# One burst instead of four for d^T g, and value products of two pairs of heads in one burst

## The chip, the cores and the metric

The kernel runs on one core of a Trainium2 chip. The metric is the device time of one execution in microseconds (us), from one launch that takes the inputs in HBM to the outputs in HBM. Everything is float32 at the interface.

## The reference

The inputs are q, k, v of 4 batches, 12 heads, 448 positions and 64 channels; three weights of a gated product (768 to 1536 and back), and a soft mixture of 8 experts with 4 slots each.

```python
scores = scale * np.matmul(q, k.transpose(0, 1, 3, 2)) - np.log(S)
attn = 1.0 / (1.0 + np.exp(-scores))
attn_out = np.matmul(attn, v)
x = attn_out.transpose(0, 2, 1, 3).reshape(B * S, H * D)
x = ((x @ w_a) * (x @ w_b)) @ w_out
logits = x @ phi
d = softmax(logits over tokens); slot_input = d.T @ x
slot_out[e] = np.maximum(slot_input[e] @ w1[e], 0.0) @ w2[e]   # 8 experts, 4 slots each
c = softmax(logits over slots)
return c @ slot_out
```

## The kernel before

The product with w_out is never formed for the tokens. With g = (x w_a) * (x w_b), the logits are g times wphi, where wphi = w_out phi is made once, and the slots' inputs are (d^T g) w_out. So for each batch the kernel needs the attention, the two products that give g (1536 rows in 12 blocks of 128, transposed: features on partitions, 448 tokens along), the logits, the softmax numerators d, and d^T g, which is added into an accumulator `acc` of 32 slots by 1536 features.

**Attention.** The generator `att` walks over 24 pairs of heads (g = 0 to 23; 6 pairs are a batch). For a pair, `emit_TK` and `emit_TQ` transpose k and q on TensorE (L144) and split each into a rounded part and a rest (h and l). `emit_S` computes the scores of a chunk of 112 keys for both heads with three products of the parts (L176), into two PSUM tiles of the tag `sc`, which has 4 buffers, and ScalarE turns each into a tile `a` with the sigmoid (L179). `emit_PV` multiplies the values of both heads with the eight tiles `a` of the pair (L189): plain float32 products of 64 columns each, the two heads beside each other in the array, into one `sc` tile. `emit_x` evacuates that tile as `xh` (ScalarE, L200) and `xl` (VectorE, L201).

**The two products.** The generator `ab` goes through 12 blocks of features of a batch. For each of w_a and w_b it runs three sets of 6 matmuls of 128 x 128 by 448 columns (L480; xh times wh, xl times wh, xh times wl) in the fp32r type, and yields after every 3 of them. There are two PSUM tiles of the tag `ab`. ScalarE copies the first product out (L489), VectorE multiplies the second with it (L492). The halves wh and wl of the weights are made ahead by VectorE (L407) and GpSimd (L408) from an f32 copy that the sync engine's queue loads (L399).

**What fills in between.** The instruction order on each engine is the order in which the code emits. While `ab` runs for batch b, `att_to` advances `att` for batch b+2 by units of cost: each `yield` of `att` says what the emitted piece counts (a transpose 430, two chunks of scores 1600, the value products 3200), and pieces are emitted while the sum lies below the share of `ab` that is done. After each set of 6 matmuls `fill_step` takes one step of the list `fill`: `group` (logits of four blocks, L443, and the transposes of g to token-major tiles `gk`, L457) and `LG` (the softmax over tokens: `logits`, L514; `tokens`, L548; then `dg`, L557). `dg` computes d^T g of the batch: for each of 4 chunks of 112 tokens, four float32 matmuls with 32 columns side by side, first over two thirds of the features (256 columns along), then over the last third (128 along). It yields after every second chunk, so a batch's d^T g stands in four pieces with a set of `ab` between them. `last_LG` does the last batch, where nothing is left to put between.

**After the products.** When `ab` of the last batch is done, the memory of its weights and inputs is opened to the loads of w_out and of the expert weights (`pump`, L688), and the expert stages run (L764 to L840).

Of the kernel before, what the change touches and what calls it, by code (L numbers as in the profile page):

```python
# [9 lines left out]
F32 = mybir.dt.float32  # L10
# [8 lines left out]
B, H, S, D = 4, 12, 448, 64  # L19
DM, FF, NS, NE, F = 768, 1536, 32, 8, 1024  # L20
C = 4
T = S // C
# [3 lines left out]
NP = H // 2  # L26
# [7 lines left out]
def body(ctx, tc, q, k, v, w_a, w_b, w_out, phi, w1, w2, out):  # L34
    nc = tc.nc
    pe, act, dve, pool, sp = nc.tensor, nc.scalar, nc.vector, nc.gpsimd, nc.sync

    const = ctx.enter_context(tc.tile_pool(name="const", bufs=1, side="left"))
    stat = ctx.enter_context(tc.tile_pool(name="stat", bufs=2, side="left"))
    ps_ctx, ab_ctx, x0_ctx, cv_ctx, at_ctx = (ctx.enter_context(ExitStack()) for _ in range(5))  # L40
    lgp = ctx.enter_context(tc.tile_pool(name="lgp", bufs=1, side="left"))
    gkp = ctx.enter_context(tc.tile_pool(name="gkp", bufs=1, side="left"))
    abp = ab_ctx.enter_context(tc.tile_pool(name="abp", bufs=1, side="left"))
# [1 line left out]
    x0p = x0_ctx.enter_context(tc.tile_pool(name="x0p", bufs=1, side="left"))  # L45
    cvp = cv_ctx.enter_context(tc.tile_pool(name="cvp", bufs=1, side="left"))
    atp = at_ctx.enter_context(tc.tile_pool(name="atp", bufs=1, side="right"))
    drp = ctx.enter_context(tc.tile_pool(name="drp", bufs=1, space=bass.MemoryType.DRAM))
    psp = ps_ctx.enter_context(tc.tile_pool(name="psp", bufs=1, space=PSUM))

# [2 lines left out]
    def ps_tile(tag, shape, bufs):  # L53
        return psp.tile(shape, F32, tag=tag, name=tag, bufs=bufs)
# [93 lines left out]
    def emit_TK(g):  # L148
        if g >= B * NP:
            return  # L150
        tk = transposed(g, "k", ms())
        if g == 0:
            tq = transposed(g, "q", ms())
        split_heads(g, "k", tk, dve.tensor_copy)
        if g == 0:
            split_heads(g, "q", tq, act.copy)

    def emit_TQ(g):
        if g >= B * NP:
            return  # L160
        split_heads(g, "q", transposed(g, "q", ms()),
                    dve.tensor_copy)
# [3 lines left out]
    def emit_S(g, chunks):  # L166

        (kh, kl), (qh, ql) = stk[g]["k"], stk[g]["q"]
        for c in chunks:
            ab = g < NP and c % 2  # L170
            sc = [ps_tile("ab" if ab else "sc", [T, S], 2 if ab else 4) for _ in range(2)]
            cs = slice(c * T, (c + 1) * T)
            for i, (kx, qx) in enumerate(((kh, qh), (kl, qh), (kh, ql))):
                for h in range(2):
                    r = slice(64 * h, 64 * h + 64)
                    pe.matmul(sc[h], kx[r, cs], qx[r], start=(i == 0), stop=(i == 2))  # L176
            for h in range(2):
                a = atp.tile([T, S], F32, tag="a", name="a", bufs=11)
                act.activation(a, sc[h], AF.Sigmoid, bias=nlog[:T], scale=1.0 / math.sqrt(D))  # L179
                a_t[g, h, c] = a  # L180

# [2 lines left out]
    def emit_PV(g, cs):  # L184
        if cs[0] == 0:
            pv_t[g] = ps_tile("sc", [128, S], 4)
        for c in cs:
            for h in range(2):
                pe.matmul(pv_t[g][64 * h:64 * h + 64], qkv_t["v", g][:, h, c, :], a_t.pop((g, h, c)),  # L189
                          start=(c == 0), stop=(c == C - 1))  # L190
# [3 lines left out]
    def emit_x(g):  # L194
        pv = pv_t.pop(g)
        qkv_t.pop(("v", g))
        b, kk = divmod(g, NP)
        xh = (x0p, x1p)[b % 2].tile([128, S], F32R, tag=f"xh{kk}", name=f"xh{kk}")
        xl = (x0p, x1p)[b % 2].tile([128, S], F32R, tag=f"xl{kk}", name=f"xl{kk}")
        act.activation(xh, pv, AF.Copy)  # L200
        dve.tensor_tensor(xl, pv, xh.bitcast(F32), op=ALU.subtract)  # L201
        xt[g] = (xh, xl)
        load_qkv(g + 3, "v")

    def att():

        emit_TK(0)
        yield 860
        for g in range(B * NP + 1):
            more = g < B * NP  # L210
            first = ((0, 1) if g == 0 else (0,) if g < NP else ()) if more else ()
            if g:
                emit_TK(g + 1)
                yield 430
            for c in first:
                emit_S(g, (c,))
                yield 800
            if g:
                emit_PV(g - 1, (0, 1, 2, 3))
                emit_x(g - 1)  # L220
                yield 3200
            elif more:
                emit_TK(g + 1)
                yield 430
            if more and g >= NP:
                emit_S(g, (0, 1))
                yield 1600
                emit_TQ(g + 1)
                yield 430
                emit_S(g, (2, 3))  # L230
                yield 1600
            elif more:
                emit_TQ(g + 1)
                yield 430
                for c in range(len(first), C):
                    emit_S(g, (c,))
                    yield 800
# [313 lines left out]
    def dg(b, dtok, gp, groups):  # L551

        gk = gtok[b, 2][:, None] if groups == (2,) else gk_01[:T].rearrange("p g (c n) -> p g c n", c=C)
        o = gp.rearrange("p (g n) -> p g n", g=3)[:, groups[0]:groups[-1] + 1]
        for c in range(C):
            for j in range(4):
                pe.matmul(o[32 * j:32 * j + 32], dtok[:, c], gk[:, :, c, j * 128:(j + 1) * 128],  # L557
                          start=(c == 0), stop=(c == C - 1))
            if c % 2:
                yield  # L560

    def LG(b):
        t = run["lsd2"] if b == B - 2 else ls_d
        run["lsd"] = t[:, :S], t[:, S:2 * S]
        dtok = t[:T, 2 * S:2 * S + C * NS].rearrange("p (c s) -> p c s", c=C)
        yield
        yield from logits(b)
        yield
        ltok = stat.tile([T, C, NS], F32, tag="ltok", name="ltok", bufs=1)
        tokens(run["lsd"][0], ltok)  # L570
        sp.dma_start(out=clog32[:, :, b], in_=ltok)
        yield
        tokens(run["lsd"][1], dtok)
        yield
        gp = ms((128, FF // 4))
        for groups in ((0, 1), (2,)):
            yield from dg(b, dtok, gp, groups)
        if b:
            dve.scalar_tensor_tensor(acc, acc, run["al"], gp, op0=ALU.mult, op1=ALU.add)
        else:  # L580
            dve.tensor_copy(acc, gp)
        yield
        if b == B - 2:
            run.pop("lsd2")
            open_slots(e1, [1])
            open_slots(gkp, [0])

    def last_LG():

        run["ms"], run["lsd"] = 0, (lps, gT_all[3])  # L590
        lg, gr = logits(B - 1), group(B - 1, 2, (act.copy, dve.tensor_copy, act.copy, act.copy))
        next(gr)
        next(lg)
        next(lg)
        next(gr)
        next(lg)
        next(gr)
        dtok = stat.tile([T, C, NS], F32, tag="ltok", name="dtok", bufs=1)
        tokens(run["lsd"][1], dtok)
        for _ in gr:  # L600
            pass
        next(lg, None)
        gp = ms((128, FF // 4))
        for groups in ((0, 1), (2,)):
            for _ in dg(B - 1, dtok, gp, groups):
                pass
        dve.scalar_tensor_tensor(acc, acc, run["al"], gp, op0=ALU.mult, op1=ALU.add)
        gt = ms((128, FF // 4))
        for gi in range(3):
            cs = slice(gi * 128, (gi + 1) * 128)  # L610
            pe.transpose(gt[:, cs], acc[:, cs], ident)
        act.copy(GT, gt)
        dve.tensor_scalar(rs, run["s"], 1e-9, None, op0=ALU.add)
        dve.reciprocal(out=rs, in_=rs)
# [99 lines left out]
    for b in range(B):  # L714
        if b == 1:
            cv_ctx.close()
        if b == B - 1:
            at_ctx.close()
            x0_ctx.close()
            e1 = ctx.enter_context(tc.tile_pool(name="e1", bufs=1, side="right"))  # L720
            run["banks"] = 1
            open_slots(e1, range(2, NE1))
            run["lsd2"] = e1.tile([128, 2048], F32, tag="e11", name="lsd2")
            run["wr"] = e1.tile([128, 2048], F32, tag="e10", name="wr")
            load_w(LAST + 2)
            load_w(LAST + 3)
        base = att_state[0]
        goal = NP * PAIR
        for i, frac in enumerate(ab(b)):
            if b < B - 1:  # L730
                att_to(base + goal * min(1.0, frac * 1.02))
            elif i % 6 == 3:
                pump()
        if b < B - 1:
            att_pairs((b + 2) * NP)
        for kk in range(NP):
            xt.pop(b * NP + kk)
        if b < B - 1:
            fill.append(LG(b))
# [39 lines left out]
    for n in range(0, len(order1), 4):  # L779
        _, g, x, _ = order1[n]  # L780
# [22 lines left out]
    for n in range(0, len(order2), 4):  # L803
        _, g, x, _ = order2[n]
# [62 lines left out]
```

## Time and profile before

| | |
|---|---|
| time, median of 3 runs (lowest to highest) | 742.64 us (740.13 to 744.14) |
| time of the profiled execution | 740.87 us |
| its span, first to last instruction | 738.8 us |
| TensorE matmul busy | 691.9 us, 94% |
| VectorE, ScalarE, GpSimd busy | 314.5, 271.4, 246.3 us |
| mean granted TensorE clock | 0.98 of full speed |

The profiled execution's own time is 2.07 us longer than its span. Times of instructions overlap on TensorE: the matmuls are pipelined, so what a stretch of matmuls costs is read from its start to the start of what follows, and not from its duration.

### The profile page before, as it was taken

To read this page: it belongs to the slowest core of one execution; us is meant where nothing else is said; L and a number is where in the kernel's file an instruction comes from. 1 tells how busy PE (TensorE), PEld (TensorE's weight loads), DVE (VectorE), ACT (ScalarE), POOL (GpSimd) and SP (SyncE) were. 2 spreads that over 40 slices of the span, in tenths; PEclk is the share of its full clock that TensorE was granted. 3 is DMA by queue.
4 is the path that set the end of the run, shared out by engine and by line. 5 is a ranking of instruction groups with operands and counts; after the bars stand their busy time and mean duration, and the time that the engine had idled before them with its cause. 6 is when DMAs were issued, how large, how long until landed. Compare 5 with 4: busy or idle time off the path is not lost.

```text
span 738.8 us, 10842 instructions
## 1 busy us (share of the span) xinstructions
PE 691.9 (94%) x4231; PEld 486.8 (66%) x4231; DVE 314.5 (43%) x452; ACT 271.4 (37%) x469; POOL 246.3 (33%) x151
## 2 busy tenths in 40 slices
PE   6999998999999999999999999999999998996682
PEld 4446767777777777777767777877888896441121
DVE  3457998899853233333333343331322232210013
ACT  4778778779643423232234222321201102110012
POOL 0006766666662322332322212322334442000000
PEclk9999999999999999999999999999999999999896
DMA  8857999899961332233323322210879927999958
GB/s 215 185 159 212 308 293 279 276 287 280 300 203 45 112 113 80 69 111 112 107 69 88 110 68 86 73 58 1 306 256 330 376 88 288 388 415 416 416 197 294
DMA packets 102930, 148.99 MB, mean 202 GB/s; under 512 B 51168, under 2 KB 76512, under 8 KB 99808
## 3 DMA queue, kind: packets, MB, share of 16 engines
q1 hardware_dynamic: 102880, 148.31, 61.3%
q8 instruction: 33, 0.54, 0.3%
q14 instruction: 17, 0.14, 0.1%
HBM read 128.46 MB, written 19.83 MB: 201 GB/s over the span
## 4 chain that ended last, share of the span: by engine, by line
PE 76%; DMA 11%; DVE 6%; ACT 4%; issue 1%; POOL 0%; SPq 0%; DVEq 0%; ACTq 0%; POOLq 0%
PE ab L480 44%; PE sc L189 9%; DMA e<-in_moe_w 7%; PE sc L176 7%; PE sc L784 3%; PE ms L144 3%; PE ms L457 2%; DVE gk L305 2%; ACT a L179 2%; PE ms L443 1%; PE ms L557 1%; DMA kn<-in_k 1%; PE ab L176 1%; DVE gk L304 1%; DMA wr_cv<-in_moe_w_a 1%
## 5 line engine op out<-in xcount | busy, mean ns | idle before, releaser
L408 POOL TENSOR_TENSOR wl<-wr_all,wh 128x768 fp32r<-128x768 f32 x50 | 92.2, 1845 | 209.1 <-DVE wh L407 159.3
L480 PE MATMUL ab<-xh,wl 128*128 128x448 f32 x576 | 144.9, 379 | 0.0
L480 PE MATMUL ab<-xh,wh 128*128 128x448 f32 x576 | 141.4, 376 | 1.4 <-ACT wh L407 1.4
L480 PE MATMUL ab<-xl,wh 128*128 128x448 f32 x576 | 135.9, 370 | 0.0
L480 PEld LDWEIGHTS ab<-xh,wh 128*128 128x128 f32 x576 | 103.4, 188 | 25.8 <-issue 15.8
L480 PEld LDWEIGHTS ab<-xh,wl 128*128 128x128 f32 x576 | 102.7, 188 | 22.4 <-issue 12.8
L179 ACT ACTIVATE a<-sc,nlog 112x448 f32<-112x448 f32 x168 | 93.7, 640 | 64.9 <-PE sc L176 64.7
L480 PEld LDWEIGHTS ab<-xl,wh 128*128 128x128 f32 x576 | 106.1, 188 | 13.5 <-issue 5.2
L310 POOL TENSOR_TENSOR w<-gk,cy 128x768 int32<-128x768 int32 x36 | 66.2, 1839 | 101.3 <-DVE gk L305 76.9
L492 DVE TENSOR_TENSOR misc<-misc,ab 128x448 f32<-128x448 f32 x48 | 29.6, 616 | 119.6 <-PE ab L480 119.6
L189 PE MATMUL sc<-a,vn 112*64 112x448 f32 x384 | 78.7, 553 | 0.0
L489 ACT COPY misc<-ab 128x448 f32<-128x448 f32 x48 | 25.9, 539 | 133.9 <-PE ab L480 133.9
L408 POOL TENSOR_TENSOR wl<-wr,wh 128x768 fp32r<-128x768 f32 x22 | 40.5, 1839 | 54.6 <-DVE wh L407 45.7
L407 DVE CAST wh<-wr_all 128x768 fp32r<-128x768 f32 x50 | 40.9, 820 | 28.9 <-issue 16.7
L189 PEld LDWEIGHTS sc<-a,vn 112*64 112x64 f32 x384 | 25.8, 139 | 41.4 <-issue 38.6
L808 PE MATMUL sc<-e,gk 128*32 128x384 f32 x240 | 37.1, 589 | 14.2 <-DMA e<-in_moe_w 13.9
L200 ACT ACTIVATE xh<-sc 128x448 fp32r<-128x448 f32 x24 | 13.1, 545 | 89.9 <-PE sc L189 89.9
L408 POOL TENSOR_TENSOR wl<-w,wh 128x768 fp32r<-128x768 f32 x24 | 44.9, 1870 | 3.1 <-ACT wh L407 3.1
L201 DVE TENSOR_TENSOR xl<-sc,xh 128x448 fp32r<-128x448 f32 x24 | 14.9, 622 | 58.9 <-ACT xh L200 58.9
L303 DVE TENSOR_SCALAR mf<-gk 128x768 f32<-128x768 f32 x36 | 34.1, 946 | 9.3 <-ACT gk L292 9.0
L808 PEld LDWEIGHTS sc<-e,gk 128*32 128x32 f32 x240 | 10.5, 125 | 39.9 <-DMA e<-in_moe_w 27.8
L176 PE MATMUL sc<-qh,kh 64*112 64x448 f32 x168 | 35.3, 415 | 0.6 <-ACT qh L137 0.6
(166 smaller groups left out, 764.7 us busy)
## 6 DMA issues: line engine op xcount, KB each, us to landing
e<-in_moe_w SPq DMA_DIRECT2D x23, 1024.0 KB, 7.3
e<-in_moe_w SPq DMA_DIRECT2D x27, 768.0 KB, 15.1
wr_all<-ab SPq DMA_DIRECT2D x50, 384.0 KB, 3.5
wr_cv<-in_moe_w_a SPq DMA_DIRECT2D x12, 768.0 KB, 6.9
wr_all<-in_moe_w_b SPq DMA_DIRECT2D x12, 768.0 KB, 7.0
wr_all<-in_moe_w_out SPq DMA_DIRECT2D x12, 768.0 KB, 7.2
ab<-w SPq DMA_DIRECT2D x24, 384.0 KB, 7.4
wr<-ab SPq DMA_DIRECT2D x22, 384.0 KB, 4.2
```

Of the source, the lines that this page charges most:

```text
L144: pe.transpose(t[:, c * T:(c + 1) * T], a[:, c].rearrange("p h d -> p (h d)"), ident[:T, :T])
L176: pe.matmul(sc[h], kx[r, cs], qx[r], start=(i == 0), stop=(i == 2))
L179: act.activation(a, sc[h], AF.Sigmoid, bias=nlog[:T], scale=1.0 / math.sqrt(D))
L189: pe.matmul(pv_t[g][64 * h:64 * h + 64], qkv_t["v", g][:, h, c, :], a_t.pop((g, h, c)), start=(c == 0), stop=(c == C - 1))
L303: dve.tensor_scalar(mf, m, LOW, HIGH, op0=ALU.max, op1=ALU.min)
L310: pool.tensor_tensor(thirds(w), m.bitcast(I32), thirds(cy_t.pop(x)), op=ALU.add)
L407: rnd(wh, t)
L408: pool.tensor_tensor(wl, t, wh.bitcast(F32), op=ALU.subtract)
L480: pe.matmul(t, w[:, kk * 128:(kk + 1) * 128], xt[b * NP + kk][xi], start=(s == 0 and kk == 0), stop=(s == 2 and kk == KD - 1))
L489: act.copy(gT_all[n % 5], t)
L492: dve.tensor_tensor(g, g, t, op=ALU.mult)
L808: pe.matmul(sps[h][32 * j:32 * j + 32], hT[:, 2 * x + i, 2 * j + g], ring[order2[n + j]][0][:, i, c0:c0 + w], start=(g == 0 and x == 0 and ...
```

## The change

Two things are changed. `dg` loses its yields: the 32 matmuls of a batch's d^T g are issued in a row. And from the pair g = 13 on, `att` emits no value products at odd g; at even g it emits those of g-2 and g-1 in a row, then both evacuations, and counts 6400. So that the eight tiles `a` of a pair can live until then, the odd pairs from 13 on take theirs from a new pool of 8 buffers (`a2`), opened when the first phase's pool `cvp` is closed.

```diff
+    more_a = {}
...
-                a = atp.tile([T, S], F32, tag="a", name="a", bufs=11)
+                a = (more_a["pool"].tile([T, S], F32, tag="a2", name="a2", bufs=8) if g >= 2 * NP and g % 2 else
+                     atp.tile([T, S], F32, tag="a", name="a", bufs=11))
...
-            if g:
+            if g > 2 * NP:
+
+                if g % 2 == 0:
+                    emit_PV(g - 2, (0, 1, 2, 3))
+                    emit_PV(g - 1, (0, 1, 2, 3))
+                    emit_x(g - 2)
+                    emit_x(g - 1)
+                    yield 6400
+            elif g:
                 emit_PV(g - 1, (0, 1, 2, 3))
                 emit_x(g - 1)
                 yield 3200
...
-            if c % 2:
-                yield
...
         for groups in ((0, 1), (2,)):
-            yield from dg(b, dtok, gp, groups)
+            dg(b, dtok, gp, groups)
...
         if b == 1:
             cv_ctx.close()
+            more_a["pool"] = ma_ctx.enter_context(tc.tile_pool(name="map", bufs=1, side="left"))
         if b == B - 1:
+            ma_ctx.close()
             at_ctx.close()
```

On TensorE the programs are the same up to the place where the value products of pair 12 stood, at the start of batch 1's `ab`. This is the order there before; numbered names are tiles, and xh, xl, wh, wl are the parts of inputs and weights.

```order
L480 MATMUL ab<-xh_2118,wh_2500 128x448
L480 MATMUL ab<-xh_2381,wh_2500 128x448
L189 MATMUL sc<-a,vn 64x448 x8
L480 MATMUL ab<-xl_942,wh_2500 128x448
L480 MATMUL ab<-xl_1214,wh_2500 128x448
L480 MATMUL ab<-xl_1527,wh_2500 128x448
```

This is TensorE's order at the first double burst now, 39 matmuls of `ab` later (L490 is the line of the products, L191 that of the value products, L567 that of d^T g).

```order
L490 MATMUL ab<-xl_1527,wh_2631 128x448
L191 MATMUL sc<-a,vn 64x448 x8
L191 MATMUL sc<-a_2643,vn 64x448
L191 MATMUL sc<-a_2645,vn 64x448
L191 MATMUL sc<-a_2655,vn 64x448
L191 MATMUL sc<-a_2657,vn 64x448
L191 MATMUL sc<-a_2712,vn 64x448
L191 MATMUL sc<-a_2714,vn 64x448
L191 MATMUL sc<-a_2724,vn 64x448
L191 MATMUL sc<-a_2726,vn 64x448
L490 MATMUL ab<-xl_1806,wh_2631 128x448
```

The eight matmuls of one pair have become sixteen in a row; the second eight read the tiles of the new pool. On TensorE, the last two pieces of d^T g of batch 0 stood like this before:

```order
L480 MATMUL ab<-xh_1805,wh_2653 128x448
L480 MATMUL ab<-xh_2118,wh_2653 128x448
L480 MATMUL ab<-xh_2381,wh_2653 128x448
L557 MATMUL ms<-gk_96,ls_d 32x128 x8
L480 MATMUL ab<-xl_942,wh_2653 128x448
L480 MATMUL ab<-xl_1214,wh_2653 128x448
L480 MATMUL ab<-xl_1527,wh_2653 128x448
L480 MATMUL ab<-xl_1806,wh_2653 128x448
L480 MATMUL ab<-xl_2119,wh_2653 128x448
L480 MATMUL ab<-xl_2382,wh_2653 128x448
L557 MATMUL ms<-gk_96,ls_d 32x128 x8
```

And all of d^T g of batch 0 stands like this now, again on TensorE:

```order
L490 MATMUL ab<-xl_1806,wh_2631 128x448
L490 MATMUL ab<-xl_2119,wh_2631 128x448
L490 MATMUL ab<-xl_2382,wh_2631 128x448
L567 MATMUL ms<-gk_95,ls_d 32x256 x16
L567 MATMUL ms<-gk_96,ls_d 32x128 x16
L490 MATMUL ab<-xh_941,wl_2632 128x448
L490 MATMUL ab<-xh_1213,wl_2632 128x448
```

The four pieces are one. On ScalarE, the evacuation of a pair stood before (here pair 13, with its last sigmoids ahead and the copy of an `ab` tile behind):

```order
L179 ACTIVATE a<-sc,nlog 112x448 x4
L489 COPY misc<-ab 128x448
L179 ACTIVATE a<-sc,nlog 112x448 x4
L200 ACTIVATE xh_2878<-sc 128x448
L489 COPY misc<-ab 128x448
```

ScalarE's order at the first double burst now:

```order
L181 ACTIVATE a_2712<-sc,nlog 112x448
L181 ACTIVATE a_2714<-sc,nlog 112x448
L181 ACTIVATE a_2724<-sc,nlog 112x448
L181 ACTIVATE a_2726<-sc,nlog 112x448
L202 ACTIVATE xh_2801<-sc 128x448
L202 ACTIVATE xh_2807<-sc 128x448
L499 COPY misc<-ab 128x448 x2
```

The two evacuations now follow each other, and the copies of `ab` tiles stand behind both.

## Rows read from the trace of the kernel before

**Rows 1.** The page's head, its second part and its chain by engine and line:
```profile
span 738.8 us, 10842 instructions
PE 691.9 (94%) x4231; PEld 486.8 (66%) x4231; DVE 314.5 (43%) x452; ACT 271.4 (37%) x469; POOL 246.3 (33%) x151
...
PE 76%; DMA 11%; DVE 6%; ACT 4%; issue 1%; POOL 0%; SPq 0%; DVEq 0%; ACTq 0%; POOLq 0%
```

**Rows 2.** Busy us by stretch: PE, PEld, DVE, ACT, POOL, clock, DMA share, GB/s:
```profile
200.00:340.00 140.00, 139.43 (x844) 102.90 (x843) 53.81 (x82) 47.12 (x84) 47.90 (x26) 1.00 0.35 104
340.00:480.00 140.00, 140.00 (x833) 105.66 (x832) 49.10 (x78) 42.52 (x78) 44.20 (x24) 1.00 0.31 92
480.00:616.00 136.00, 136.00 (x756) 113.79 (x754) 36.58 (x62) 20.30 (x38) 51.52 (x28) 1.00 0.56 199
623.00:626.00 3.00, 2.82 (x65) 1.85 (x64) 0.11 (x1) 0.76 (x2) 2.06 (x13) 1.00 1.02 429
640.00:650.00 10.00, 10.00 (x99) 3.04 (x92) 0.00 (x0) 0.53 (x1) 0.00 (x0) 1.00 1.01 417
```

**Rows 3.** All waits of PE between 200 and 618 us: line, waited for, us, times, longest:
```profile
PE ms L335 <- ACT wT L336: 0.6, 1, 0.6
```

**Rows 4.** Timeline of PE around one pair's value products: start, us, engine, line, operation:
```profile
357.00 0.85 PE L480 MATMUL ab<-xh,wl 128*128 128x448 f32 x3
357.78 3.23 PE L189 MATMUL sc<-a,vn 112*64 112x448 f32 x16
360.94 0.87 PE L480 MATMUL ab<-xh,wl 128*128 128x448 f32 x3
361.65 1.38 PE L480 MATMUL ab<-xh,wh 128*128 128x448 f32 x6
362.87 1.38 PE L480 MATMUL ab<-xl,wh 128*128 128x448 f32 x6
```

**Rows 5.** The same burst cut off at 358.5 and at 359.2 us:
```profile
357.78 0.97 PE L189 MATMUL sc<-a,vn 112*64 112x448 f32 x4
357.78 1.72 PE L189 MATMUL sc<-a,vn 112*64 112x448 f32 x8
```

**Rows 6.** Timeline of PE, d^T g of batch 0 in its four pieces:
```profile
253.36 1.07 PE L557 MATMUL ms<-gk,ls_d 112*32 112x256 f32 x16
254.37 0.88 PE L480 MATMUL ab<-xh,wl 128*128 128x448 f32 x3
...
256.20 1.07 PE L557 MATMUL ms<-gk,ls_d 112*32 112x256 f32 x16
257.20 0.86 PE L480 MATMUL ab<-xh,wh 128*128 128x448 f32 x3
...
260.20 0.64 PE L557 MATMUL ms<-gk,ls_d 112*32 112x128 f32 x16
260.77 1.48 PE L480 MATMUL ab<-xl,wh 128*128 128x448 f32 x6
262.18 0.64 PE L557 MATMUL ms<-gk,ls_d 112*32 112x128 f32 x16
262.75 1.49 PE L480 MATMUL ab<-xh,wl 128*128 128x448 f32 x6
```

**Rows 7.** Timeline of PE, d^T g of the last batch, already in one piece:
```profile
623.02 2.81 PE L557 MATMUL ab<-gk,dtok 112*32 112x256 f32 x64
```

**Rows 8.** Timeline of ACT around the value products of Rows 4; brackets give idle time before:
```profile
353.02 2.21 ACT L179 ACTIVATE a<-sc,nlog 112x448 f32<-112x448 f32 x4 [4.04 <-PE sc L176]
...
361.08 0.55 ACT L200 ACTIVATE xh<-sc 128x448 fp32r<-128x448 f32 x1 [5.43 <-PE sc L189]
```

**Rows 9.** The queue's waits (SP) from 500 us to the end:
```profile
SPq L399 <- PE ab L480: 22.2, 1, 22.2
```

**Rows 10.** The chain that ended last, in order of time, its late part:
```profile
594.47 21.89 PE ab L480 x108
...
660.02 15.04 DMA e<-in_moe_w
```

More of the change, by code (lines that the diff above doesn't have):

```diff
@@ L39, in body @@
     stat = ctx.enter_context(tc.tile_pool(name="stat", bufs=2, side="left"))
-    ps_ctx, ab_ctx, x0_ctx, cv_ctx, at_ctx = (ctx.enter_context(ExitStack()) for _ in range(5))
+    ps_ctx, ab_ctx, x0_ctx, cv_ctx, ma_ctx, at_ctx = (ctx.enter_context(ExitStack()) for _ in range(6))
     lgp = ctx.enter_context(tc.tile_pool(name="lgp", bufs=1, side="left"))
@@ L604, in last_LG @@
         for groups in ((0, 1), (2,)):
-            for _ in dg(B - 1, dtok, gp, groups):
-                pass
+            dg(B - 1, dtok, gp, groups)
         dve.scalar_tensor_tensor(acc, acc, run["al"], gp, op0=ALU.mult, op1=ALU.add)
```

## The prediction

> **What bounds the kernel now.** I read the page's head and its chain first. TensorE is busy for 691.9 us of a span of 738.8 us, and 76% of the chain that ended last is its matmuls [rows 1]. Everything that the change touches lies between the start of batch 1's products (pair 12's value products) and the first blocks of the last batch (d^T g of batch 2). So I took the table of busy time by stretch next: from 200 to 616 us TensorE is busy for 139.4 of 140, 140 of 140 and 136 of 136 us, at a granted clock of 1.00, while VectorE, ScalarE and GpSimd are each busy for at most 54 us of any of these stretches [rows 2]. The list of its waits from 200 to 618 us has a single entry, 0.6 us [rows 3]. So in this stretch nothing is waited for: whatever TensorE is spared there, the end comes earlier by, as long as no new wait arises. And whatever is to be spared must lie inside "busy" time, since there is no idle time.
>
> That it does is seen in the timeline, read from start to start. Six matmuls of the products that stand inside a long run take 1.22 us (361.65 to 362.87), 0.203 us each [rows 4]. Three of them that stand between a transpose and a burst of value products take 0.78 us (357.00 to 357.78) where 0.61 would do, and the first three behind that burst take 0.71 us (360.94 to 361.65) [rows 4]. Six that stand between two pieces of d^T g take 1.41 us (260.77 to 262.18) where 1.22 would do [rows 6]. So a stretch of the products that is cut out by other work costs 0.17 to 0.19 us more than its matmuls: about 0.10 us on entering it, the rest on leaving it. The bursts have a fixed part too, below.
>
> What follows the products is tied to them. The queue that loads the last expert weights waits for a matmul of the products, once for 22.2 us [rows 9], and the chain goes from the products (594.47 us) to the transfers of the expert weights, whose first link in it begins at 660.02 us [rows 10]. Those transfers are the bound at the end, but they are let go by TensorE, so they start earlier by what it is spared; I count no loss there.
>
> **The change, part by part.** *d^T g in one burst, three times* (batches 0 to 2; the last batch had no work between its pieces before). The four pieces of batch 0 take 1.01, 1.00, 0.57 and 0.57 us from start to start, 3.15 us [rows 6]. What one burst takes is in the trace, because the last batch does the same 64 records in one: 2.81 us of duration [rows 7], at a clock of 1.00 [rows 2]. A piece's duration is some 0.06 us more than its start-to-start time (1.07 against 1.01, [rows 6]), so I take 2.75 us: 0.40 us less per batch, 1.2 us for three. This term has no lower bound of its own, since the operation was seen.
>
> *Value products of two pairs in one burst, six times* (pairs 12 to 23, twelve bursts become six). Cut off at two points, the burst shows 4 records after 0.97 us, 8 after 1.72 and 16 after 3.23 us [rows 4, 5]; from 8 to 16 records that is 0.378 us per two (one of each head), so eight of those are 3.02 us. The burst takes 3.16 us from start to start (357.78 to 360.94) [rows 4], hence a fixed part of 0.14 us, and a double burst should take about 6.18 us instead of 6.32. Six times 0.14 is 0.84 us. The trace has no two pairs behind each other: if the second pair pays its own beginning, this is nothing; at the rate of the first eight records (1.72 less 0.97 us for four, 3.00 us in all [rows 5]) the fixed part is 0.16 us, 0.96 us for six. I take 0.84, since within a burst the rate does not change when a new chunk starts.
>
> *The stretches between.* Taking out six bursts and nine pieces would join fifteen pairs of stretches. But the rest of the attention now falls at other places between the sets. So I counted in the two orders: 166 stretches of the products between other work before, 153 now, 13 fewer with the same number of matmuls. At 0.18 us each, the middle of what the rows show, that is 2.34 us. If only the entering cost goes (0.10 us), it is 1.3 us; with all fifteen at 0.19 us it is 2.85 us.
>
> *What the delay costs elsewhere.* Delaying an even pair's value products by one pair keeps eight more `a` tiles alive, for which there is the new pool. In the order, from the last scores of a pair to the burst that needs them lie 21 matmuls of the products at every double burst; before there were 18 or 21. Moreover the burst begins with the older pair, so the younger pair's sigmoids have some 3 us more. Before, the last four sigmoids ended at 355.23 us (353.02 and 2.21) and the burst began at 357.78 [rows 4, 8]: 2.5 us to spare, over 5 now. Between scores and scores there are 18 or 21 matmuls, as before, so the four `sc` buffers are turned over no faster; a double burst takes two of them and, by its 6400 units, leaves as much of the products behind it as two single ones. The loads of v come in twos behind the burst and have a pair's time before they are wanted. The sync engine's queue puts nothing of its own ahead of them that TensorE waits for. I cost all this at nothing. If that cover were gone, a late tile of sigmoids would cost up to one sigmoid pass of four, 2.2 us [rows 8], at each burst.
>
> The sum: 1.2 + 0.84 + 2.34 = 4.4 us. Its bounds are 1.2 + 0 + 1.3 = 2.5 us and 1.2 + 0.96 + 2.85 = 5.0 us. The profiled execution took 740.87 us (span 738.8 and 2.07 around it), so an execution like it would take 736.5. The median of the three runs, 742.64, lies 1.8 us above that execution; the forecast for a median is 742.64 - 4.4 = **738.2 us**, with 737.6 to 740.1 from the bounds.
>
> **The rivals.** *Half of it.* The second pair of a burst pays its own beginning and a seam costs only its entry: 2.5 us, 740.1 us, within what can be told from no change (about 0.5%, 3.7 us). For it speaks that 13 seams at 0.18 are an average of differing neighbours, and that the double burst is not in the trace. Against it speaks that leaving the products towards a burst was measured apart from entering (0.78 for three matmuls in front of the burst, 0.71 behind it [rows 4]).
>
> *Nothing.* A seam might cost nothing in truth, the extra time being one of how the records' starts are put down, so that it reappears elsewhere; then only order changes, and the time stays at about 742.6 us. Against it: the extra tenths add up in a span that has no idle time, and the one-piece d^T g is shorter than the four by 0.40 us in the same trace [rows 6, 7]. The Trainium skill, "TensorE: Matmul & The Clock Gate", section "Step-by-step: what each phase is for", says that the drain of one matmul overlaps the fill of the next, so that matmuls in a stream follow each other at the pace of their columns; taken for any two matmuls, that makes every seam free and this rival true, with a sum of 0 where the rows give 4.4. This trace disagrees where the shape or type changes: 1.41 us in place of 1.22 [rows 6]. The same skill's "TensorEngine Tiling (Array Packing)", section "Key Properties", says that a change of tiling mode drains the engine, which is nearer to what these rows show.
>
> *Slower.* ScalarE takes its instructions in order. The evacuations of both pairs now stand one behind the other, and copies of `ab` tiles stand behind them; during a double burst ScalarE is held for some 6 us. If the copy of a tile is among what is held, TensorE finds no free `ab` tile after the burst and waits until the second evacuation (0.55 us) and the copy (0.55 us) are done [rows 8], some 1.2 us with the signals; at six bursts that is 7.2 us, less the 4.4 gained: 745.4 us. Against it: ScalarE sat idle for 5.43 us ahead of the evacuation before [rows 8], and with two `ab` tiles TensorE has a tile of 18 matmuls, 3.7 us, to fill before it needs the copy. It decides only if the copy is later than that.
>
> *More.* All fifteen seams go at 0.19 us and some of the scores' own seams with them: a little above 5 us, 737.4 us.
>
> **How the numbers follow.** Forecast 0.61, more 0.08, half of it 0.20, nothing 0.05, slower 0.06. The three runs before lie from 2.5 us below their median to 1.5 us above, and another median of few runs may be off by some 2 us. The range takes the case of more and the forecast's upper bound and lets each reach out by this: 735.6 to 741.6 us; it leaves out the slower case, half of the case of nothing, and little of the rest. Faster by over 0.5% has the first two cases, 0.69; within 0.5% the next two, 0.25; slower 0.06.
>
> **What would show it.** In the profile after: a burst of 32 records of value products of about 6.18 us from start to start; d^T g of 64 records of 2.75 us three times; still no wait of TensorE of note between 200 and 618 us; the end of the products and the first transfers of expert weights earlier by 4 to 5 us; the stretch of the last stages as long as before. It is wrong if the sum of waits on TensorE in this stretch grows by more than 1 us, if the double burst takes 6.3 us, or if TensorE reaches the end of the products earlier and the tail gives it back.

## The result and the profile after

The changed kernel took 735.3 us in the median of 8 runs (734.06 to 737.01), the kernel before 740.99 us (739.62 to 744.14) beside it: a ratio of 0.9913, 95% interval 0.9887 to 0.9939. Two later comparisons of the same kernels gave 0.9939 (0.9915 to 0.9964) and 0.9922 (0.9903 to 0.9941). It is faster, as forecast; 735.3 us lies 0.3 us below the stated range. The medians of the changed kernel in the two later comparisons were 736.25 us, inside that range, and 735.54 us, just below it. The profiled execution has a span of 732.1 us, 6.7 us less than before.

The page's head and its chain by engine, after, against [rows 1]:

```profile
span 732.1 us, 10834 instructions
PE 684.2 (93%) x4231; PEld 488.1 (67%) x4231; DVE 311.5 (43%) x452; ACT 271.9 (37%) x469; POOL 246.4 (34%) x151
...
PE 75%; DMA 13%; DVE 5%; ACT 3%; POOL 1%; issue 1%; SPq 0%; DVEq 0%; ACTq 0%; POOLq 0%
```

TensorE does the same 4231 matmul records in 7.7 us less busy time. Its waits from 200 to 609 us, after, against [rows 3]:

```profile
PE ms L345 <- ACT wT L346: 0.6, 1, 0.6
```

So no new wait came in. The bursts, in the timeline of TensorE after (start, us, engine, line, operation), against [rows 4, 6]:

```profile
250.33 6.23 PE L191 MATMUL sc<-a,vn 112*64 112x448 f32 x32
256.50 0.88 PE L490 MATMUL ab<-xl,wh 128*128 128x448 f32 x3
257.31 2.81 PE L567 MATMUL ms<-gk,ls_d 112*32 112x256 f32 x64
260.05 1.49 PE L490 MATMUL ab<-xh,wl 128*128 128x448 f32 x6
```

The double burst goes from 250.33 to 256.50: 6.17 us for 32 records, where 6.18 was forecast and two singles took 6.32. The d^T g of batch 0 goes from 257.31 to 260.05: 2.74 us for 64 records where the four pieces took 3.15.

To see where the time went, I cut both executions at work that stands at the same place in both programs, the first logits matmuls of the third group (third visit of L443, L453 after) and of the last group. The four rows are from the timelines, two of before and then two of after.

```profile
226.93 0.96 PE L443 MATMUL ms<-misc,wphi 128*32 128x448 f32 x8
616.29 1.79 PE L443 MATMUL ms<-misc,wphi 128*32 128x448 f32 x8
```

```profile
225.27 0.96 PE L453 MATMUL ms<-misc,wphi 128*32 128x448 f32 x8
609.77 1.79 PE L453 MATMUL ms<-misc,wphi 128*32 128x448 f32 x8
```

Between these places, **the stretch** from here on, lie all changed instructions. (A stretch *of the products* is something else, here as in the prediction: matmuls of the products in a row with no other work between.) It took 616.29 - 226.93 = 389.36 us before and 609.77 - 225.27 = 384.50 us after: 4.86 us less. The other 1.9 us of the spans' difference come from work that the change does not touch: 1.66 us ahead of the stretch, 0.2 us behind it (732.1 - 609.77 = 122.3 us follow it after, 122.5 before). Ahead of it, the order of TensorE is the same in both programs. Two windows near the start show one part of that (busy us of PE, PEld, DVE, ACT, POOL, then granted clock, DMA share, GB/s), before and then after:

```profile
24.00:26.00 2.00, 2.00 (x8) 0.70 (x8) 1.97 (x3) 1.67 (x3) 0.00 (x0) 0.50 1.30 200
26.00:28.00 2.00, 2.00 (x12) 0.72 (x10) 1.31 (x2) 0.00 (x0) 0.50 (x1) 0.79 0.63 89
```

```profile
24.00:26.00 2.00, 2.00 (x12) 0.58 (x9) 1.93 (x3) 0.64 (x2) 0.00 (x0) 1.00 1.06 163
26.00:28.00 2.00, 2.00 (x18) 1.36 (x16) 1.52 (x4) 1.05 (x2) 1.57 (x1) 1.00 0.28 47
```

In the execution before, the clock stood at the lower of its two levels here for some 3 us (0.50, which is 1.2 GHz), and one burst of value products took 4.47 us, where the same burst took 3.23 us in the execution after, whose clock stayed at the higher level. That is 1.24 of the 1.66 us. Up to the fall, TensorE was busy for 1.66 and 1.39 of 2 us (20 to 24 us). In the execution after it was busy for 1.82 and 1.28 of 2 us at about the same place of the order (18 to 22 us), and the clock stayed, so these rows do not tell why it fell.

The stretch by kind of work, each from its start to the start of what follows, summed over the starts of the matmul records, in us, with the number of pieces of that kind in brackets:

| | before | after | difference | forecast |
|---|---|---|---|---|
| products (L480) | 277.85 (109) | 275.13 (96) | -2.72 | -2.34 |
| value products (L189) | 37.89 (12) | 36.98 (6) | -0.90 | -0.84 |
| d^T g (L557) | 9.45 (12) | 8.21 (3) | -1.24 | -1.20 |
| scores, transposes, logits, the rest | 64.17 | 64.17 | 0.00 | 0 |
| sum | 389.36 | 384.50 | -4.86 | -4.38 |

### The profile page after: what moved, and what is told of

Its sections match the earlier page's. It is cut to its first block, busy times and chain, and to the rows that moved or that the text cites. A ratio compares the mean times of both kernels' runs of the same rounds, so it can differ in the third digit from the quotient of the medians.

```text
span 732.1 us, 10834 instructions
## 1 busy us (share of the span) xinstructions
PE 684.2 (93%) x4231; PEld 488.1 (67%) x4231; DVE 311.5 (43%) x452; ACT 271.9 (37%) x469; POOL 246.4 (34%) x151
## 4 chain that ended last, share of the span: by engine, by line
PE 75%; DMA 13%; DVE 5%; ACT 3%; POOL 1%; issue 1%; SPq 0%; DVEq 0%; ACTq 0%; POOLq 0%
PE ab L490 44%; PE sc L191 9%; DMA e<-in_moe_w 7%; PE sc L177 7%; PE sc L793 3%; PE ms L145 3%; PE ms L467 2%; DMA wr_cv<-in_moe_w_a 2%; DVE gk L315 2%; PE ms L453 1%; PE ab L177 1%; PE ms L567 1%; DMA wr_all<-in_moe_w_b 1%; DMA out<-w 1%; DMA kn<-in_k 1%
## 5 line engine op out<-in xcount | busy, mean ns | idle before, releaser
L490 PE MATMUL ab<-xh,wh 128*128 128x448 f32 x576 | 142.1, 377 | 1.4 <-ACT wh L417 1.4
L490 PE MATMUL ab<-xh,wl 128*128 128x448 f32 x576 | 141.8, 376 | 0.0
L490 PE MATMUL ab<-xl,wh 128*128 128x448 f32 x576 | 136.2, 371 | 0.0
L490 PEld LDWEIGHTS ab<-xh,wh 128*128 128x128 f32 x576 | 103.3, 188 | 20.9 <-issue 10.9
L490 PEld LDWEIGHTS ab<-xh,wl 128*128 128x128 f32 x576 | 104.1, 188 | 18.2 <-issue 8.6
L490 PEld LDWEIGHTS ab<-xl,wh 128*128 128x128 f32 x576 | 106.0, 188 | 15.4 <-issue 7.3
L191 PE MATMUL sc<-a,vn 112*64 112x448 f32 x384 | 76.1, 544 | 0.0
L191 PEld LDWEIGHTS sc<-a,vn 112*64 112x64 f32 x384 | 26.0, 137 | 41.5 <-issue 38.7
L417 DVE CAST wh<-wr_all 128x768 fp32r<-128x768 f32 x50 | 35.2, 704 | 37.1 <-POOL wl L418 22.9
```

Of the source, the lines that this page charges most:

```text
L417: rnd(wh, t)
L490: pe.matmul(t, w[:, kk * 128:(kk + 1) * 128], xt[b * NP + kk][xi], start=(s == 0 and kk == 0), stop=(s == 2 and kk == KD - 1))
```

## The experiments

Three theories stood against each other. **A**: the saving is made of seams and of beginnings of bursts, 4.9 us, and the rest of the difference is chance at the start. A *seam* is a place where other work is put between the products: TensorE leaves them and enters them again, and both can cost time. **B**: the start got faster by the changed program. **C**: the gain has another cause than the seams.

### The kernel before, again

No edit.

> The kernel before, unchanged, profiled once more. Theory A (the change saves 4.9 us after 227 us, and the other 1.7 us between the two profiled executions is the granted clock near the start, which differs from one execution to the next): the stretch from the third L443 (227 us) to the last one (616 us) again takes 389.4 us within 0.3 us, while the time of the third L443 may lie anywhere from 224.5 to 228 us, earlier when the clock shows no half level around 24 us. Theory B (the changed program makes the start faster by its layout): the third L443 comes at 226.9 us within 0.3 us again, with the half level around 24 us again.

The stretch went from 225.58 to 614.94 us: 389.36 us, the same to the hundredth. The third L443 came 1.35 us earlier than in the first profile, and around 24 us the clock was at its full level; it fell later instead, so that its mean was 0.97 between 60 and 120 us. B falls for the start: the same program begins differently from one execution to the next.

### The changed kernel, again

No edit; run in two groups, as after_again and after_third.

> The changed kernel, unchanged, profiled once more and timed. Theory A (seams and burst beginnings save 4.9 us; the start is chance): 389.36 - 4.86 = 384.5 us from the third to the last L443-line matmuls within 0.3 us; ratio to before about 0.9935 (736.2 us where before has 741), and below that only by what the start gives in a given run. Theory B (the start is faster by the program's layout): third such matmul at 225.3 us within 0.3 again, ratio about 0.991.

> The changed kernel once more, on the same chip as merge_t and merge_tg, for their comparison: 384.5 us within 0.1 in the stretch, a ratio to before of 0.9935 or a little below, and the parts before and behind the stretch differing from its other two profiles by some us.

The stretches took 384.50 us both times (224.86 to 609.36, and 226.50 to 611.00). The third such matmuls lay at 225.27, 224.86 and 226.50 us in the three profiles. The medians were 736.25 us (ratio 0.9939, 0.9915 to 0.9964) and 735.54 us (0.9922, 0.9903 to 0.9941). A holds: 1 - 4.86/741 = 0.9934 lies in all three intervals.

### Only d^T g in one burst

```diff
-            if c % 2:
-                yield
...
-            yield from dg(b, dtok, gp, groups)
+            dg(b, dtok, gp, groups)
```

> Only d^T g in one burst; value products as before. The order has 157 stretches of the products against 166. Theory A (each seam about 0.2 us, each burst has a beginning): 3 x 0.41 + 9 x 0.2 = 3.0 us less in the stretch from the third to the last L443-line matmuls, 386.4 us; ratio about 0.996. Rival C (the gain is made by the double bursts of value products alone, for instance by earlier evacuation): no change, 389.4 us and ratio 1.000.

The stretch took 386.38 us (227.74 to 614.12), 2.98 us less; d^T g took 8.21 us, 1.24 less, and the products 1.78 us less at 9 seams fewer, 0.20 us each. The median was 737.8 us, the ratio 0.9943 (0.9917 to 0.9968). A was right to 0.02 us, and C fell in this form: part of the gain comes without any double burst of value products.

### Only the value products of two pairs in one burst

The changed kernel, with the two parts of the edit above undone.

> Only the value products of two pairs in one burst; d^T g in four pieces as before. The order has 162 stretches of the products against 166, since more places of the attention fall apart from each other. Theory A (seams and beginnings): 6 x 0.15 + 4 x 0.2 = 1.7 us less in the stretch from the third to the last L443-line matmuls, 387.7 us; ratio about 0.9977. Rival C (the gain is made by the double bursts alone): 4.9 us less, 384.5 us. With dg_only, A wants the two savings to add to 4.9 us within 0.3.

The stretch took 387.16 us (229.74 to 616.90), 2.20 us less: 0.90 in the value products, 1.27 in the products, 0.02 in the rest. The median was 738.98 us, the ratio 0.9965 (0.9941 to 0.9989). A's 1.7 us was 0.5 too small, and the two parts sum to 5.18 us, 0.28 above the 4.9 that A gave and at the edge of what it allowed.

Four seams fewer gave 1.27 us in place of 0.8, so not all of this is a price per seam. The starts of the records tell the two things apart. In the middle of most stretches of the products a matmul takes 0.2027 us up to the start of the next. What the first matmul of a stretch takes above that is counted here as entering, what the last one takes above it as leaving, and what the others take above it as *inside*. These are the differences to the kernel before, summed over the stretch, in us:

| difference to before | after | dg_only | pv_only | split (next section) |
|---|---|---|---|---|
| entering, behind work on part of the array | -1.36 (13 fewer) | -0.94 (9 fewer) | -0.45 (4 fewer) | +2.14 (20 more) |
| leaving, towards such work | -1.21 (13 fewer) | -0.86 (9 fewer) | -0.36 (4 fewer) | +2.04 (22 more) |
| inside | -0.16 | +0.02 | -0.50 | +0.12 |

Work on part of the array is all other work but the transposes of q, k and g and the three matmul pieces of L514. Entries behind those, and leavings towards them, stayed the same in number, except for two leavings fewer in split, and changed the sums by no more than 0.04 us. So an entry costs 0.10 to 0.11 us and a leaving 0.09 to 0.10 in all four, four seams are worth the 0.8 us that A gave, and the surplus of 0.5 us lies inside the stretches of the products.

There the long ones, of 12 matmuls or more, take one of two paces and keep it to their end: 202.3 to 203.1 ns per matmul, or 206.6 to 206.8. Before, 294 matmuls stood in stretches at the slower pace, here only 150: 144 of them at 4 ns are 0.58 us. In the changed kernel they are 234, in dg_only 288, which is why the two parts sum to more than the whole. The pace does not belong to a place in the program. The last two long stretches, of 120 and of 108 matmuls, have the same neighbours in both programs and stand in the chain that ended last. This is the first of them before (the second, of 21.89 us, is in [rows 10]), and then both of them after:

```profile
561.96 24.79 PE ab L480 x120
```

```profile
555.49 24.32 PE ab L490 x120
587.53 22.31 PE ab L490 x108
```

The one of 120 matmuls became faster by 0.47 us (206.7 to 202.7 ns each), the one of 108 slower by 0.42 us (21.89 to 22.31). The repeated profiles of both programs show the same two durations to the hundredth. What gives a stretch its pace when it is entered stays open.

### The opposite: twice as many bursts

On the kernel before:

```diff
-            if c % 2:
-                yield
+            yield
...
-                emit_PV(g - 1, (0, 1, 2, 3))
-                emit_x(g - 1)
-                yield 3200
+                if g > 2 * NP:
+                    emit_PV(g - 1, (0, 1))
+                    yield 1600
+                    emit_PV(g - 1, (2, 3))
+                    emit_x(g - 1)
+                    yield 1600
+                else:
...
```

> The opposite of the change, on the kernel before: d^T g of a batch in eight pieces instead of four, and from pair 12 on the value products of a pair in two halves. In the stretch from the third to the last L443-line matmuls the order has 129 stretches of the products against 109, 78 of them ending at work that uses part of the array's columns or rows against 56, and 24 more beginnings of bursts. Theory A (entering 0.09 to 0.10 us, leaving towards such work 0.09, a beginning 0.14 to 0.15): 20 x 0.1 + 22 x 0.09 + 24 x 0.145 = 7.4 us more, 396.8 us against 389.4; ratio about 1.010. Rival (the seams cost nothing, the savings come from another effect of the later value products): within 1 us of 389.4, ratio 1.000.

The stretch took 397.16 us (226.76 to 623.92), 7.80 us more where A said 7.4. The median was 748.03 us, the ratio 1.0086 (1.0057 to 1.0116). The timeline of TensorE shows a half of value products and one of the eight pieces of d^T g:

```profile
260.05 1.50 PE L487 MATMUL ab<-xl,wh 128*128 128x448 f32 x6
261.48 0.64 PE L564 MATMUL ms<-gk,ls_d 112*32 112x256 f32 x8
262.05 1.50 PE L487 MATMUL ab<-xh,wl 128*128 128x448 f32 x6
...
264.21 0.85 PE L487 MATMUL ab<-xh,wh 128*128 128x448 f32 x3
264.99 1.72 PE L189 MATMUL sc<-a,vn 112*64 112x448 f32 x8
266.64 0.86 PE L487 MATMUL ab<-xh,wh 128*128 128x448 f32 x3
```

A half burst goes from 264.99 to 266.64: 1.65 us, and two of them 3.30, where the whole took 3.16. Six matmuls of the products between pieces take 1.43 us (260.05 to 261.48) in place of 1.22. The sum over the stretch is 39.70 us of value products (+1.81, 0.15 for each of 12 beginnings), 11.11 of d^T g (+1.66, 0.14 for each of 12), and 282.16 of products (+4.31). Of this 4.31 us, 4.18 are entries and leavings (the table above). An entry, a leaving and a beginning cost the same, to a hundredth or two, when they are added as when they are taken out, so the rival falls.

### Transposes behind the scores

On the changed kernel, to see whether fewer seams give more:

```diff
                 emit_S(g, (0, 1))
-                yield 1600
+                if g < 2 * NP - 1:
+                    yield 1600
                 emit_TQ(g + 1)
-                yield 430
+                yield 430 if g < 2 * NP - 1 else 2030
                 emit_S(g, (2, 3))
-                yield 1600
+                if g >= 2 * NP - 1:
+                    emit_TK(g + 2)
+                yield 1600 if g < 2 * NP - 1 else 2030
...
-                emit_TK(g + 1)
-                yield 430
+                if g < 2 * NP:
+                    emit_TK(g + 1)
+                    yield 430
```

> The changed kernel, and from pair 11 on the transposes of q and k directly behind two chunks of scores, with no set of the products between (their cost counted with the scores). 82 stretches of the products against 96, with as many (43) that end at work on part of the array. Theory A: 14 entries at 0.09 to 0.10 us, 1.3 us less than the changed kernel: 383.2 us in the stretch. Rival (transposes behind scores wait for a free ms buffer, or scores' own leaving cost stays and the transposes gain nothing): 384.5 us or more, with a wait of TensorE on the line of the transposes.

The stretch took 383.03 us (225.25 to 608.28), 1.47 us less than the changed kernel's, and no wait of TensorE is listed in it. The median was 734.40 us, ratio to before 0.9909 (0.9886 to 0.9933), against 735.54 (0.9922) for the changed kernel in the same group. In the stretch A was right to 0.2 us in the sum, but not in the parts: the products took 1.79 us less, the transposes of q and k took 0.68 us more, now that they stand behind scores, and those of g 0.39 us less. The two intervals overlap, so the run times alone do not tell the two kernels apart; the stretches do.

### Two transposes of g in one step

On top of that:

```diff
             evac[c](gk[:, c], tp)
-            yield
+            if c % 2:
+                yield
```

> merge_t, and the transposes of g in two steps of two chunks instead of four steps of one. 64 stretches of the products against 82. Theory A: 18 entries at 0.09 us, 1.6 us less than merge_t: 381.6 us in the stretch, if the two ms buffers are free. Rival (two chunks in a step need both ms buffers, which then also the attention's transposes want): waits of TensorE on the lines of the transposes for an evacuation, and 383 us or more.

The stretch took 384.76 us (226.88 to 611.64), 1.73 us more than merge_t. The median was 736.06 us, the ratio 0.9932 (0.9911 to 0.9953). A's number was wrong here and the rival's mechanism came in. The waits of TensorE from 226 to 612 us:

```profile
PE ms L471 <- DVE kl L139: 1.2, 3, 0.4
PE sc L563 <- ACT lsd L551: 0.5, 1, 0.5
```

and a place in its timeline:

```profile
328.07 0.86 PE L495 MATMUL ab<-xh,wl 128*128 128x448 f32 x3
328.77 0.60 PE L471 MATMUL ms<-ident,misc 128*112 128x128 f32 x4
329.77 0.62 PE L471 MATMUL ms<-ident,misc 128*112 128x128 f32 x4 [0.40 <-DVE kl L139]
330.14 1.46 PE L495 MATMUL ab<-xh,wh 128*128 128x448 f32 x6
331.44 1.03 PE L471 MATMUL ms<-ident,misc 128*112 128x128 f32 x8
332.24 1.46 PE L495 MATMUL ab<-xl,wh 128*128 128x448 f32 x6
```

The second chunk's transposes wait for VectorE, which still holds a buffer with the transposed keys. The products did take 1.12 us less than in merge_t, but the transposes of g took 2.87 us more (16.34 against 13.47), of which the waits listed on their line are 1.2 us. Without a listed wait, eight records go from 331.44 to 332.24, 0.80 us, and two single steps took 0.35 each: what a seam between a transpose and the products would give back is lost between two steps of transposes here. What takes that 0.10 us was not tried.

## Why the prediction was wrong in its number and right in its mechanism

**What bounds.** Right. TensorE has no wait of note in the stretch, before and after, and all that it was spared there came through: the last stages begin earlier by no less than that. The first link of transfers in the chain after, against [rows 10]:

```profile
652.88 15.06 DMA e<-in_moe_w
```

That is 7.14 us earlier than 660.02, of which 6.52 were already there at the last logits: the 4.86 of the stretch and the 1.66 from the start.

**d^T g.** Forecast 1.20, measured 1.24 us. The single burst of the last batch told the price of the others.

**Value products.** Forecast 0.84, measured 0.90 us. The second pair pays no beginning of its own.

**The stretches between.** Forecast 2.34, measured 2.72 us. This term was mis-sized. The count of 13 was right, but 0.18 us was the middle of two rows, and the row that gave 0.17 has a transpose ahead of the products. The 13 seams that went all stood between pieces of work on part of the array, as in the row that gave 0.19. Such a seam costs 0.106 us on entering and 0.093 on leaving in the starts of the records, 13 of them 2.57 us. The other 0.16 us lies inside the stretches of the products and goes with their pace (see pv_only), which the prediction did not have. That it came to no more is chance as far as the prediction goes: with the value products alone it was 0.50.

**Cover.** Right that no wait replaces the gain. After the first double burst ScalarE's row of evacuations is short, as its timeline after shows (brackets: idle time ahead), against [rows 8]:

```profile
245.80 2.21 ACT L181 ACTIVATE a<-sc,nlog 112x448 f32<-112x448 f32 x4
253.61 0.54 ACT L202 ACTIVATE xh<-sc 128x448 fp32r<-128x448 f32 x1 [5.59 <-PE sc L191]
256.64 0.55 ACT L202 ACTIVATE xh<-sc 128x448 fp32r<-128x448 f32 x1 [2.49 <-PE sc L191]
261.57 0.53 ACT L499 COPY misc<-ab 128x448 f32<-128x448 f32 x1 [4.38 <-PE ab L490]
```

The sigmoids end at 248.01 us, 2.3 us ahead of the burst and 5.3 us ahead of the part that needs them. The first evacuation is done inside the burst. The copy of the next tile comes 4.4 us later, and it waits for TensorE: the slower rival needed the opposite. At the other five bursts TensorE has no listed wait either.

**The rivals.** *Half of it* fell: the gain in the stretch is 4.86, not 2.5 us. *Nothing* fell by split, where more seams made the stretch 7.8 us longer. The rule that stood for it (the Trainium skill, "TensorE: Matmul & The Clock Gate", section "Step-by-step: what each phase is for") says that the drain of one matmul overlaps the fill of the next. The trace does not bear it out for matmuls of one kind behind those of another: six matmuls between pieces of d^T g took 1.43 us in split, and 1.22 inside a long stretch of the products before. *More* forecast a little above 5 us, and 4.86 lies between it and the forecast.

**The step that failed** is the one from the sum to a median, "742.64 - 4.4 = 738.2 us". It took the median of three runs as the base and let the range reach out by 2 us. In the three comparisons the kernel before had medians of 740.99 (8 runs), 741.65 (26 runs, 735.24 to 745.63) and 741.47 us (11 runs). From 741 the same sum of 4.4 us gives 736.6, and 4.86 gives 736.1. The base was about 1 to 1.6 us too high, the sum 0.48 us too small, 0.38 of it in the stretches between, and both errors point the same way. The prediction had worked out 736.5 us for an execution like the profiled one, and set it aside for the median. The remaining 0.8 us (736.1 to 735.3) is put down to the parts outside the stretch, since the stretch took 384.50 us in all three profiles; those parts differ between executions: the stretch began at 224.86 to 229.74 us in the ten profiles here, though only merge_t and merge_tg change anything ahead of it, and little. The other two comparisons of the changed kernel have medians of 736.25 and 735.54. Whether some tenths of the 0.8 us are a lasting effect of the change is not settled; the intervals of the ratios, which all hold 0.9934, do not ask for one.

## What to carry to other kernels

Where TensorE has no idle time, read its timeline from start to start: a piece of work that is cut into a stream of other matmuls costs its own beginning, here 0.14 to 0.15 us, and a seam in the stream, here 0.20 us when both of its sides are work on part of the array. Price a seam from a row with the same neighbours. The sum over a count of seams from the order came out 0.02 to 0.5 us off here, but for merge_tg, where a wait came in. Merging pays where the merged pieces do not share a short supply of buffers; with two buffers between two transposes, the seam saved was lost to a wait and to the second step of transposes. And a forecast of a sub-percent change is best stated as a difference, since the median of three runs of the kernel before was off by a fifth to a third of the effect.

## What was not expected of the hardware

The stretch took the same time in every repeated profile of a program (389.36 twice, 384.50 three times), while the same program took from 224.86 to 226.50 us to reach it (three profiles of the changed kernel); in these profiles the spread comes from the part ahead of the stretch and from what follows, not from the dense middle. In the middle, leaving the products for a transpose of q, k or g cost nothing that the starts show (0.002 us in the mean before), and entering them behind one 0.085 us. Leaving them for work on part of the array cost 0.09 us, and entering them behind it 0.106. A long stretch of the same matmuls, at a granted clock of 1.00 throughout, ran at about 202.7 or about 206.7 ns per matmul, from its third matmul to its end.
